# The high part of the first network's weights: written by VectorE behind its bit operation instead of by ScalarE

## The chip, the cores and the metric

One core of a Trainium2 chip runs the whole program in one launch. The metric is the device time of that launch in microseconds (us); the time before is the median of three runs, 988.29 us (987.73 to 989.37). Engines are named as the profile names them: PE (TensorE matmul), PEld (TensorE weight load), DVE (VectorE), ACT (ScalarE), POOL (GpSimd) and SP (SyncE, which only issues DMAs here).

## The reference

Attention over 4 batches of 8 heads, 576 positions and 64 features, is computed in two parts and added: over a window of 3 neighbours on either side, and over the means of 4 positions. The result `x` (2304 tokens by 512) goes through two networks:

```python
def _moe_ref(x, w_in, w_out):
    h = x @ w_in                # 512 -> 2048
    g = h * np.cos(h)
    return (g @ w_out)          # 2048 -> 512

def _moe2_ref(x, w_a, w_b, w_out):
    a = x @ w_a                 # 512 -> 1536
    b = x @ w_b
    return (a * b @ w_out)
```

Inputs and outputs are float32, and the output has to be near that in accuracy.

## The kernel before

**Products of split numbers.** TensorE multiplies in a shorter format (`F32R`) here, so each operand is split into a high part (a copy rounded to `F32R`) and a low part (what is left). `mm3` (lines 430 to 432) issues three matmuls per product: high by high, high by low, low by high.

**The first network** runs over token blocks of 288 (two of 432 at the end) and sixteen slices `f` of 128 hidden features. One step `g` of the main loop is one slice of one block: `h_mm` multiplies a slice of `w_in` with the block (12 matmuls into one of two PSUM buffers with the tag `h`), `cos_a` (lines 469, 470) and `cos_b` (474, 477, 478) make h·cos(h) in `gs`, `split_hi` (482, ACT) and `split_lo` (486, POOL for the first steps, DVE later) split it, and three steps behind `back_mm` multiplies it with a slice of `w_out` (12 matmuls into the accumulators `acc`). The cosine is a chain of five instructions that changes engines: ACT 469, DVE 470, ACT 474 (a sine), ACT 477 (a square), DVE 478. Line 478 is the last reader of the PSUM buffer, so the `h` matmuls of two steps later wait for it.

**The first network's weights** arrive once, in 32 slices of 128 x 512 (16 of `w_in`, 16 of `w_out`), as 8-byte numbers, and are turned into float32 on the core. For each slice `to_f32` issues two ACT instructions (lines 113 and 116) and one DVE bit operation (118, a shift and an or, which writes the float32 bit pattern `lw`); then `wsplit` writes the high part into `t[:, 0]` (line 125) and POOL subtracts for the low part (126). `lw` is every other 4-byte word of the slice's buffer. The main loop asks for slices by `goal(g)`: four before the first step, then two in each of the first seven steps, then slower, until all are there after step 23. The load of a slice waits for line 118 of the slice eight places ahead of it.

**Beside it runs attention** for the next block: DVE makes sums of four (190) and masked scores (228, 232, 233, 246), ACT takes exponentials (247, 255, 257, 262), DVE and POOL normalise (285 to 303), PE transposes (310, 319) and multiplies (329, 336).

**The order of the work.** Each engine runs its instructions in one fixed order. The program is written step by step, but the Tile framework chooses that order when it builds the kernel, by its own schedule; another instruction on an engine moves its neighbours too. From the last block of the first network on, the program's own order is kept. The second network (a Strassen-like product of splits of `w_a`, `w_b`, `w_out2`) fills the time from about 575 us to the end; the 24 slices of its weights that are prepared earlier go through `to_f32` as well, but not through `wsplit`.

Of the kernel before, what the change touches and what calls it, by code (L numbers as in the profile page):

```python
# [9 lines left out]
F32 = mybir.dt.float32  # L10
# [5 lines left out]
AF = mybir.ActivationFunctionType  # L16
# [51 lines left out]
def kernel(ctx, tc, qT, kT, vw, vds, w_in, w_out, w_a, w_b, w_out2, out):  # L68
    nc = tc.nc
    pe, act, dve, pool, sp = nc.tensor, nc.scalar, nc.vector, nc.gpsimd, nc.sync  # L70
# [40 lines left out]
    def to_f32(raw, out=None, behind=None):  # L111
        lw, hh = raw[:, :, 0], raw[:, :, 1]
        ins = act.activation(out=hh.bitcast(F32), in_=hh.bitcast(F32), func=AF.Prelu, scale=2.0 ** -112, alpha=2.0 ** 32)
        after(ins, behind)
        top = raw.rearrange("p f e -> p (f e)").bitcast(mybir.dt.uint8).rearrange("p (f b) -> p f b", b=8)[:, :, 3]
        ins = act.activation(out=lw, in_=top, func=AF.Identity, scale=1.0 / 32.0, bias=down[:, :1])
        after(ins, behind)
        ins = dve.scalar_tensor_tensor(out=lw if out is None else out, in0=hh, scalar=3, in1=lw, op0=ALU.logical_shift_left, op1=ALU.bitwise_or)  # L118
        marks.append(ins.ins)
        return lw  # L120

    def wsplit(raw, lo_eng):
        t = wp.tile([128, 2, 512], F32R, tag="w", name="w", bufs=33)
        lw = to_f32(raw)
        act.activation(out=t[:, 0], in_=lw.bitcast(F32), func=AF.Copy)
        lo_eng.tensor_tensor(out=t[:, 1], in0=lw.bitcast(F32), in1=t[:, 0].bitcast(F32), op=ALU.subtract)  # L126
        return t[:, 0], t[:, 1]

# [289 lines left out]
    def split_to(nm, f):  # L418
        while (nm, f) not in wts:
            key = stream[pos[1]]  # L420
            while pos[0] < len(stream) and pos[0] < pos[1] + C["AHEAD"]:
                load_next()
            wts[key] = wsplit(raws.pop(key), pool)
            pos[1] += 1
# [89 lines left out]
    if True:  # L514
# [227 lines left out]
        for g in range(NG + LAG):  # L742
            if g < NG:
                i, u, f = seq[g]
                if g == NG - NF:
                    at_ctx.close()
                    p2 = ctx.enter_context(tc.tile_pool(name="p2", bufs=1))
                    act, dve, pool = InOrder(tc, act), InOrder(tc, dve), InOrder(tc, pool)
# [289 lines left out]
```

## Time and profile before

| what | value |
|---|---|
| median of three runs | 988.29 us |
| the profiled execution's own time | 987.76 us |
| its span (first to last instruction) | 985.6 us |
| PE busy | 942.4 us (96%) |
| PE weight load busy | 892.4 us (91%) |
| DVE busy | 708.1 us (72%) |
| ACT busy | 609.9 us (62%) |
| POOL busy | 477.5 us (48%) |
| mean granted clock of TensorE | 0.979 of full speed |

The shares are means over the whole span. The stages differ much: the lines that the change touches run only in the first 160 us. "Busy" of PE counts a matmul from its start to its modelled end, so that PE is not necessarily at its peak where it is busy. "Idle before" of an engine is put down to the instruction that released it.

### The profile page before, as it was taken

To read this page: it belongs to the slowest core of one execution; us is meant where nothing else is said; L and a number is where in the kernel's file an instruction comes from. 1 tells how busy PE (TensorE), PEld (TensorE's weight loads), DVE (VectorE), ACT (ScalarE), POOL (GpSimd) and SP (SyncE) were. 2 spreads that over 40 slices of the span, in tenths; PEclk is the share of its full clock that TensorE was granted. 3 is DMA by queue.
4 is the path that set the end of the run, shared out by engine and by line. 5 is a ranking of instruction groups with operands and counts; after the bars stand their busy time and mean duration, and the time that the engine had idled before them with its cause. 6 is when DMAs were issued, how large, how long until landed. Compare 5 with 4: busy or idle time off the path is not lost.

```text
span 985.6 us, 18933 instructions
## 1 busy us (share of the span) xinstructions
PE 942.4 (96%) x6828; PEld 892.4 (91%) x6828; DVE 708.1 (72%) x1378; ACT 609.9 (62%) x1399; POOL 477.5 (48%) x615
## 2 busy tenths in 40 slices
PE   4888899999999999999999999999999999999998
PEld 3767898989889989899999989998999998999998
DVE  7677777577767777656346878889856789667773
ACT  5689897476675858676468765555444455444452
POOL 3757642014221351112015347658777769566682
PEclk8779999999999999999999999999999999999999
DMA  9646511244546363432049855576554685753431
GB/s 287 244 132 209 189 43 39 69 126 138 157 125 184 116 185 113 123 105 60 1 138 280 253 181 193 188 288 238 222 173 154 205 340 214 256 176 141 160 134 49
DMA packets 98829, 163.30 MB, mean 166 GB/s; under 512 B 6960, under 2 KB 64816, under 8 KB 98736
## 3 DMA queue, kind: packets, MB, share of 16 engines
q1 hardware_dynamic: 98736, 162.10, 49.7%
q8 instruction: 54, 0.88, 0.4%
q14 instruction: 39, 0.32, 0.1%
HBM read 128.25 MB, written 33.82 MB: 164 GB/s over the span
## 4 chain that ended last, share of the span: by engine, by line
PE 73%; DVE 10%; ACT 6%; DMA 5%; POOL 4%; issue 2%; SPq 0%; POOLq 0%; DVEq 0%; ACTq 0%
PE z L431 12%; PE z L432 12%; PE z L430 12%; PE h L430 5%; PE acc L430 5%; PE h L431 5%; PE h L432 5%; PE acc L432 5%; PE acc L431 5%; DMA vs<-in_vds_dram 2%; PE att L336 2%; PE att L217 1%; PE att L244 1%; POOL vd L183 1%; PE att L329 1%
## 5 line engine op out<-in xcount | busy, mean ns | idle before, releaser
L64 POOL TENSOR_TENSOR sb<-w,sb 128x256 fp32r<-128x256 f32 x154 | 120.7, 796 | 90.7 <-ACT sb L64 87.0
L430 PE MATMUL h<-xh,w 128*128 128x288 f32 (+1 forms) x448 | 146.7, 327 | 7.9 <-DVE gs L478 7.0
L430 PE MATMUL acc<-gh,w 128*128 128x288 f32 (+1 forms) x448 | 145.0, 325 | 2.0 <-DVE ev L463 1.0
L431 PE MATMUL acc<-gl,w 128*128 128x288 f32 (+1 forms) x448 | 142.3, 318 | 1.9 <-POOL gl L486 1.7
L432 PE MATMUL h<-xh,w 128*128 128x288 f32 (+1 forms) x448 | 142.1, 317 | 1.2 <-POOL w L126 1.2
L431 PE MATMUL h<-xl,w 128*128 128x288 f32 (+1 forms) x448 | 142.9, 319 | 0.0
L432 PE MATMUL acc<-gh,w 128*128 128x288 f32 (+1 forms) x448 | 141.9, 317 | 0.0
L64 ACT ACTIVATE sb<-w 128x256 fp32r<-128x256 f32 x252 | 96.4, 415 | 66.1 <-PE z L432 54.2
L430 PEld LDWEIGHTS h<-xh,w 128*128 128x128 f32 x448 | 85.6, 191 | 15.5 <-DVE gs L478 9.9
L432 PE MATMUL z<-xh,sb 128*128 128x384 f32 x288 | 97.4, 338 | 0.2 <-POOL sb L64 0.2
L430 PE MATMUL z<-xh,sb 128*128 128x384 f32 x288 | 96.9, 336 | 0.4 <-issue 0.4
L431 PE MATMUL z<-xl,sb 128*128 128x384 f32 x288 | 97.2, 338 | 0.0
L430 PEld LDWEIGHTS acc<-gh,w 128*128 128x128 f32 x448 | 85.1, 190 | 7.7 <-issue 2.9
L618 POOL TENSOR_TENSOR praw<-praw 128x128 f32<-128x128 f32 x24 | 12.8, 531 | 162.3 <-DVE praw L118 128.5
L431 PE MATMUL z<-gl,w 128*128 128x384 f32 x252 | 85.7, 340 | 4.4 <-DVE gl L64 4.1
L431 PEld LDWEIGHTS acc<-gl,w 128*128 128x128 f32 x448 | 85.2, 190 | 4.0 <-POOL gl L486 2.1
L432 PEld LDWEIGHTS h<-xh,w 128*128 128x128 f32 x448 | 86.0, 192 | 2.8 <-POOL w L126 1.5
L431 PEld LDWEIGHTS h<-xl,w 128*128 128x128 f32 x448 | 85.8, 192 | 1.9 <-issue 0.9
L432 PEld LDWEIGHTS acc<-gh,w 128*128 128x128 f32 x448 | 85.0, 190 | 2.4 <-issue 1.1
L430 PE MATMUL z<-gh,w 128*128 128x384 f32 x252 | 85.1, 338 | 0.1
L432 PE MATMUL z<-gh,w 128*128 128x384 f32 x252 | 84.9, 337 | 0.0
L64 DVE TENSOR_TENSOR sb<-w,sb 128x256 fp32r<-128x256 f32 x98 | 62.2, 637 | 26.5 <-ACT sb L64 26.4
(141 smaller groups left out, 2503.6 us busy)
## 6 DMA issues: line engine op xcount, KB each, us to landing
w<-wd SPq DMA_DIRECT2D x63, 512.0 KB
w<-wd_a SPq DMA_DIRECT2D x18, 512.0 KB
w<-wd_b SPq DMA_DIRECT2D x18, 512.0 KB
raw<-in_w_in_dram SPq DMA_DIRECT2D x16, 512.0 KB
raw<-in_w_out_dram SPq DMA_DIRECT2D x16, 512.0 KB
w<-wd_a SPq DMA_DIRECT2D x18, 384.0 KB
w<-wd_b SPq DMA_DIRECT2D x18, 384.0 KB
praw<-in_w_a_dram SPq DMA_DIRECT2D x12, 512.0 KB
```

The source lines that it names most:

```text
L64: return lambda *a, **k: self.tc.keep_in_program_order(f(*a, **k))
L183: pool.tensor_tensor(out=o, in0=t[:, :, 0], in1=t[:, :, 1], op=ALU.add)
L217: pe.matmul(p[r, W * w:W * w + W], qt[u, hp][r, off:off + W], kt[b, hp][r, BASE[half] + off:BASE[half] + off + W], start=not pem, stop=True,)
L244: pe.matmul(p[a][:QD, :SD], qd[u, hp][r, :], kd[b, hp][r, :], start=True, stop=True)
L329: pe.matmul(p[64 * a:64 * a + 64, NB:NB + QD], vdt[b, hp][:, a, c], pd[u, hp][:, 2 * a + c], start=(c == 0), stop=(c == 1),)
L336: pe.matmul(p[64 * a:64 * a + 64, xo:xo + n], vt[u, hp // 2][r, w, a], pt[u, hp // 2][r, w, 64 * a + qo:64 * a + qo + n], start=True, stop ...
L430: i = pe.matmul(ps_out, lh, rh, start=start, stop=False, skip_group_check=more)
L431: pe.matmul(ps_out, lh, rl, start=False, stop=False, skip_group_check=more)
L432: pe.matmul(ps_out, ll, rh, start=False, stop=stop, skip_group_check=more)
L618: pool.tensor_tensor(out=s1, in0=a21, in1=a22, op=ALU.add)
```

## The change

One line of `wsplit`: the high part is written by a DVE copy and not by an ACT activation.

```diff
     def wsplit(raw, lo_eng):
         t = wp.tile([128, 2, 512], F32R, tag="w", name="w", bufs=33)
         lw = to_f32(raw)
-        act.activation(out=t[:, 0], in_=lw.bitcast(F32), func=AF.Copy)
+        dve.tensor_copy(out=t[:, 0], in_=lw.bitcast(F32))
         lo_eng.tensor_tensor(out=t[:, 1], in0=lw.bitcast(F32), in1=t[:, 0].bitcast(F32), op=ALU.subtract)
         return t[:, 0], t[:, 1]
```

The copy is called CAST in the lists of instructions. 32 instructions leave ACT, and 32 come to DVE. Since the framework chooses the order anew, instructions beside them move on all engines: the order differs from about 29 us to about 165 us of the profile before, and not behind that.

ACT, from the first step's line 469 to its line 477 (the first cosine chain; `raw` are weight slices, `smd` scores of the means). Before:

```order
L469 ACTIVATE gs<-h 128x288
L247 ACTIVATE smd<-att,mxd 72x144
L113 ACTIVATE raw<-raw 128x512
L125 ACTIVATE w<-raw 128x512
L247 ACTIVATE smd<-att,mxd 72x144
L474 ACT_TABLE_LOAD
L474 ACTIVATE gs<-gs 128x288
L125 ACTIVATE w<-raw 128x512
L477 ACTIVATE gs<-gs 128x288
```

Now:

```order
L469 ACTIVATE gs<-h 128x288
L247 ACTIVATE smd<-att,mxd 72x144
L474 ACT_TABLE_LOAD
L474 ACTIVATE gs<-gs 128x288
L247 ACTIVATE smd<-att,mxd 72x144
L477 ACTIVATE gs<-gs 128x288
```

Two instructions of line 125 and one of line 113 no longer stand inside the chain (113 has moved ahead of it).

DVE, from line 470 to line 478 of the same chain. Before:

```order
L470 SCALAR_TENSOR_TENSOR gs<-gs,h 128x288
L233 TENSOR_TENSOR smx<-smx,mx 128x5x64
L118 SCALAR_TENSOR_TENSOR raw<-raw 128x512
L228 TENSOR_TENSOR smx<-att,mask 128x5x64
L232 TENSOR_REDUCE mx<-smx 128x5
L228 TENSOR_TENSOR smx<-att,mask 128x5x64
L233 TENSOR_TENSOR smx<-smx,mx 128x5x64
L232 TENSOR_REDUCE mx<-smx 128x5
L246 TENSOR_REDUCE mxd<-att 72x1
L233 TENSOR_TENSOR smx<-smx,mx 128x5x64
L478 SCALAR_TENSOR_TENSOR gs<-gs,h 128x288
```

Now:

```order
L470 SCALAR_TENSOR_TENSOR gs<-gs,h 128x288
L233 TENSOR_TENSOR smx<-smx,mx 128x5x64
L246 TENSOR_REDUCE mxd<-att 72x1
L125 CAST w<-raw 128x512
L228 TENSOR_TENSOR smx<-att,mask 128x5x64
L118 SCALAR_TENSOR_TENSOR raw<-raw 128x512
L232 TENSOR_REDUCE mx<-smx 128x5
L228 TENSOR_TENSOR smx<-att,mask 128x5x64
L478 SCALAR_TENSOR_TENSOR gs<-gs,h 128x288
```

One copy has come between them; two of line 233 and one of line 232 have gone behind line 478.

DVE, the normalising of the second block's scores, which lies between lines 470 and 478 of the third step. Its beginning, before:

```order
L470 SCALAR_TENSOR_TENSOR gs<-gs,h 128x288
L118 SCALAR_TENSOR_TENSOR raw<-raw 128x512 x2
L190 TENSOR_REDUCE kd<-k 128x144 x2
L285 TENSOR_REDUCE sl<-smx 128x10 x2
L286 TENSOR_SCALAR sl<-sl 128x10
```

Now:

```order
L470 SCALAR_TENSOR_TENSOR gs<-gs,h 128x288
L125 CAST w<-raw 128x512
L118 SCALAR_TENSOR_TENSOR raw<-raw 128x512
L125 CAST w<-raw 128x512
L118 SCALAR_TENSOR_TENSOR raw<-raw 128x512 x2
L285 TENSOR_REDUCE sl<-smx 128x10 x2
```

Two copies and one more bit operation stand ahead of line 285; two sums of line 190 have gone behind it. Its end, before:

```order
L303 TENSOR_TENSOR smd<-smd,sd 72x288
L190 TENSOR_REDUCE kd<-k 128x144
L297 TENSOR_SCALAR sd<-sd 72x2
L298 RECIPROCAL sd<-sd 72x2
L303 TENSOR_TENSOR smd<-smd,sd 72x288
L297 TENSOR_SCALAR sd<-sd 72x2
L298 RECIPROCAL sd<-sd 72x2
L303 TENSOR_TENSOR smd<-smd,sd 72x288
L478 SCALAR_TENSOR_TENSOR gs<-gs,h 128x288
```

Now:

```order
L125 CAST w<-raw 128x512
L298 RECIPROCAL sd<-sd 72x2
L190 TENSOR_REDUCE kd<-k 128x144
L303 TENSOR_TENSOR smd<-smd,sd 72x288
L297 TENSOR_SCALAR sd<-sd 72x2
L125 CAST w<-raw 128x512
L298 RECIPROCAL sd<-sd 72x2
L190 TENSOR_REDUCE kd<-k 128x144
L303 TENSOR_TENSOR smd<-smd,sd 72x288
L125 CAST w<-raw 128x512
L190 TENSOR_REDUCE kd<-k 128x144
L478 SCALAR_TENSOR_TENSOR gs<-gs,h 128x288
```

Four copies (three of them here, one two rows ahead) have come between the norms, and the next step's line 470 as well, four rows ahead of the piece; one sum of line 190 has gone behind line 478. Up to that line 478 the program now has written twelve high parts.

## Rows read from the trace of the kernel before

**Rows 1.** Busy time by stretch: from:to, length, then PE, PEld, DVE, ACT, POOL, PEclk, DMA.

```profile
0.00:30.00 30.00, 16.48 (x175) 12.71 (x176) 20.56 (x57) 16.59 (x46) 14.72 (x30) 0.76 0.94 306
30.00:68.00 38.00, 32.55 (x281) 25.62 (x279) 26.77 (x59) 29.16 (x72) 23.59 (x31) 0.74 0.48 166
68.00:98.00 30.00, 26.02 (x287) 23.73 (x286) 20.13 (x38) 28.39 (x64) 22.04 (x21) 1.00 0.62 200
98.00:165.00 67.00, 61.26 (x486) 57.24 (x486) 50.48 (x103) 58.34 (x134) 36.06 (x42) 0.97 0.29 91
165.00:985.60 820.60, 806.13 (x5610) 773.13 (x5608) 590.16 (x1122) 477.40 (x1088) 381.05 (x494) 1.00 0.50 165
...
50.00:59.50 9.50, 9.50 (x34) 7.55 (x34) 5.87 (x13) 6.40 (x14) 1.81 (x3) 0.50 0.73 245
```

**Rows 2.** What PE waited for from 68 to 98 us: total us, times, longest.

```profile
PE h L430 <- DVE gs L478: 3.2, 2, 2.1
PE h L432 <- POOL w L126: 0.6, 1, 0.6
```

**Rows 3.** Groups by form of ACT, 30 to 165 us: count, busy us, mean ns, idle before.

```profile
L116 ACT ACTIVATE raw<-raw,down 128x512 uint32<-128x512 uint8 x28 | 21.4, 766 | 0.1
L125 ACT ACTIVATE w<-raw 128x512 fp32r<-128x512 f32 x32 | 21.4, 672 | 3.2 <-DVE raw L118 2.3 <-POOL w L126 0.7
L113 ACT ACTIVATE raw<-raw 128x512 f32<-128x512 f32 x27 | 18.3, 679 | 0.0
```

**Rows 4.** Line 118 on DVE, 30 to 165 us: ns min/median/max.

```profile
L118 DVE SCALAR_TENSOR_TENSOR raw<-raw x28: 673/694/2165, 32.6 to 157.2; 128x512 uint32<-128x512 uint32 x28
```

**Rows 5.** Groups by form of DVE, 30 to 165 us.

```profile
L190 DVE TENSOR_REDUCE kd<-k 128x144 f32<-128x576 f32 x4 | 2.9, 737 | 0.0
L190 DVE TENSOR_REDUCE qd<-q 128x72 f32<-128x288 f32 x4 | 1.7, 442 | 0.0
L286 DVE TENSOR_SCALAR sl<-sl 128x10 f32<-128x10 f32 x4 | 0.6, 160 | 0.0
```

**Rows 6.** ACT in order of time, first cosine chain: start us, us, [idle before].

```profile
41.31 0.67 ACT L113 ACTIVATE raw<-raw 128x512 f32<-128x512 f32 x1
41.87 0.66 ACT L125 ACTIVATE w<-raw 128x512 fp32r<-128x512 f32 x1
...
44.46 0.66 ACT L125 ACTIVATE w<-raw 128x512 fp32r<-128x512 f32 x1
45.03 0.43 ACT L477 ACTIVATE gs<-gs 128x288 f32<-128x288 f32 x1
```

**Rows 7.** DVE in order of time, the same chain and the third step's.

```profile
41.35 0.44 DVE L470 SCALAR_TENSOR_TENSOR gs<-gs,h 128x288 f32<-128x288 int32 x1
41.71 1.39 DVE L233 TENSOR_TENSOR smx<-smx,mx 128x320 f32<-128x320 f32 x1
...
47.16 0.44 DVE L478 SCALAR_TENSOR_TENSOR gs<-gs,h 128x288 f32<-128x288 f32 x1
...
55.92 0.44 DVE L470 SCALAR_TENSOR_TENSOR gs<-gs,h 128x288 f32<-128x288 int32 x1
...
67.48 0.44 DVE L478 SCALAR_TENSOR_TENSOR gs<-gs,h 128x288 f32<-128x288 f32 x1
```

**Rows 8.** PE in order of time, what follows the two lines 478.

```profile
47.65 0.40 PE L430 MATMUL h<-xh,w 128*128 128x288 f32 x1 [1.53 <-DVE gs L478]
...
67.99 0.80 PE L336 MATMUL att<-smx,v 64*64 64x57 f32 x20
68.72 0.40 PE L430 MATMUL h<-xh,w 128*128 128x288 f32 x1
```

**Rows 9.** What PE waited for from 98 to 165 us.

```profile
PE h L430 <- DVE gs L478: 1.7, 2, 1.1
PE acc L431 <- POOL gl L486: 1.6, 1, 1.6
PE att L244 <- DVE smx L228: 1.0, 1, 1.0
```

**Rows 10.** POOL's line 126 over the span: duration ns min/median/max, and what POOL waited for.

```profile
L126 POOL TENSOR_TENSOR w<-raw,w x32: 1287/1318/1772, 33.5 to 158.7; 128x512 fp32r<-128x512 f32 x32
...
  ACT w L125: 20.5, 14
```

**Rows 11.** DVE and POOL in order of time around 117 us.

```profile
116.57 2.17 DVE L118 SCALAR_TENSOR_TENSOR raw<-raw 128x512 uint32<-128x512 uint32 x1 [0.21 <-DMA raw<-in_w_in_dram]
...
116.88 1.31 POOL L126 TENSOR_TENSOR w<-raw,w 128x512 fp32r<-128x512 f32 x1
```

## The prediction

> **What bounds the kernel now.** I read the busy time by stretch first, because the changed line runs only between 31 and 158 us. Behind 165 us PE is busy 806.1 of 820.6 us [rows 1]: that part is PE's own, the order there is unchanged, and it can only start sooner or later. So the question is how much sooner or later the stretch from 30 to 165 us ends. I cut it in three: I from 30 to 68 us, II from 68 to 98, III from 98 to 165. PE stands idle 5.5 us in I, 4.0 in II and 5.7 in III (length less busy, [rows 1]), 15.2 us together; no gain there can be larger, but for the clock, below. In II the engine that is busiest is not PE but ACT, 28.4 of 30 us, and next comes what PE waits for in that stretch: 3.2 us for line 478, the end of the cosine chain, and 0.6 us for a low part of the weights [rows 2]. Three of the chain's five instructions run on ACT and stand there in line behind weight conversion. In III ACT is 87% busy and DVE 75%; in I neither leads all the time.
>
> **What leaves ACT.** 32 instructions of 672 ns, 21.4 us [rows 3]: nine each in I and II, fourteen in III. ACT's waits in front of them (2.3 us for line 118) go with them. POOL, which waited 20.5 us for them [rows 10], now waits for DVE's copy instead; it has time.
>
> **What comes to DVE.** 32 copies of 128x512 float32 words. No row of before shows such a copy between two places of SBUF. The nearest is line 118, DVE's own pass over the same 512 words, 694 ns at the median [rows 4]; I take 0.69 us. A second row agrees: the reductions of line 190 take 442 ns for 288 words and 737 ns for 576 [rows 5], 1.02 ns a word, so 512 would take 0.67 us. The lower end is what an instruction costs that does nearly nothing, 0.16 us for ten words (line 286, [rows 5]). The upper end is 0.69 us plus a whole instruction of POOL, 1.32 us [rows 10], 2.0 us, which is near the longest line 118, 2165 ns [rows 4]. At 0.69 us DVE gets 22.1 us. The Trainium skill ("VectorE: DVE Perf Modes", the perf-mode tier table) says that a float32 copy within SBUF may run two words a cycle, and its cost table gives about 0.33 us for 512 words, an estimate; by it DVE would get 10.5 us and the sum below would be 5.3 us of gain and not 3.2. No row here shows that rate.
>
> **Stretch I.** The first cosine chain loses two of line 125 and one of line 113 on ACT. From start to start these take 1.1 us ahead of the table load and 0.57 us ahead of line 477 (41.31 to 42.4, 44.46 to 45.03, [rows 6]). So ACT's part ends 1.7 us sooner, at 43.8. DVE's part now holds line 233 (1.39 us, [rows 7]), one of 246, one copy, two of 228, one of 118 and one of 232 between lines 470 and 478: with 0.69 each for the copy and 118, 0.3 to 0.5 for the rest and some 0.08 of overlap, 4.2 us from 41.7, so line 478 starts at 45.9 and not at 47.16 [rows 7]. PE waited 1.53 us for it [rows 8] and starts 1.3 us sooner: **-1.3 us**.
>
> Then comes a part in which DVE alone sets the pace: from line 470 at 55.92 to line 478 at 67.48 [rows 7] it normalises scores. Into it come six copies (4.1 us), one more line 118 (0.7) and one line 470 (0.4), and one line 190 (0.7) leaves: 4.5 us more. It starts 1.3 us sooner, so this line 478 moves from 67.48 to 70.7. PE did not wait for it before: it was at line 336 until 68.7, and the next `h` matmul began at 68.72 [rows 8], 0.8 us behind the end of line 478. Now that matmul is late: 70.7 and 0.4 for the instruction make 71.1, **+2.4 us**. The cover (attention's matmuls on PE) is gone there. Stretch I together: +1.1 us.
>
> **Stretch II.** Nine copies' worth of work leaves ACT, 6.0 us. By the new order twelve high parts, not nine, are written by line 478 of the third step, so three slices less are converted here: 3 x (0.68 + 0.77) us less on ACT [rows 3], three of line 118 less on DVE, and six copies instead of nine. ACT: 28.4 - 6.0 - 4.3 = 18.0 us. DVE: 20.1 + 6 x 0.69 - 3 x 0.69 = 22.2 us. PE, 26.0 us [rows 1], becomes the busiest, and its waits (3.8 us, [rows 2]) have little left to wait for. I take 3.3 of its 4.0 idle us, since five steps in this stretch still hand over from engine to engine: **-3.3 us**; ends 0 and -4.0.
>
> **Stretch III.** ACT falls by 9.4 to 48.9 us, DVE rises by 9.7 to 60.1 of 67 us: DVE now has the share (90%) that ACT had. PE waits 1.7 us for line 478, 1.6 for a low part on POOL and 1.0 for scores on DVE [rows 9]. The last two gain nothing from a lighter ACT. I take **-1.0 us** of the first; ends +2 and -2.7.
>
> **Loads** cost nothing: their issue waits on line 118 of an earlier slice, and that line's own wait for data in the whole stretch is 0.2 us [rows 11].
>
> Sum: +1.1 - 3.3 - 1.0 = -3.2 us. The profiled execution took 987.76 us, 0.53 below the median of 988.29; taken from the median, **985.1 us**.
>
> **The rivals.** *A, the sum above, likeliest.* Its own range is 981 to 987.5.
>
> *B, a cheap copy and a full PE.* If the copy costs near its lower end of 0.16 us, the normalising part grows by 1.4 us and starts 1.3 sooner, so stretch I keeps its -1.3; II gives all of its 4.0 and III 2.3: -7.6 us, 980.7. Beyond it lies the clock: from 50 to 59.5 us it was granted at 0.50, the lower of its two levels (1.2 of 2.4 GHz), against 1.00 in II [rows 1]; a PE with shorter waits ahead of that might keep the upper one for longer. For it: PE's longest waits hang on ACT's queue. Against: no copy so cheap is in the trace.
>
> *C, the load only changes engines.* DVE takes 22 us where ACT loses 21, the chain of five waits in one line instead of the other, and nothing moves: 988.3. For it: in III DVE ends at ACT's old share. Against: in II the two do not balance, 22.2 against 28.4 us.
>
> *D, slower: the copy and POOL's subtraction lock each other out.* Line 118 at 116.57 took 2.17 us instead of 0.69, and POOL's line 126 ran inside it, 1.31 us [rows 11]: DVE instructions with such operands wait for POOL's to end. The copy's consumer is just this line 126, started when the copy ends, with the next line 118 or copy right behind on DVE. DVE's 97.4 us of 30 to 165 (26.8 + 20.1 + 50.5, [rows 1]) and 22.1 for copies make 119.5 of 135; at a packing of 95% (ACT's in II) DVE binds from 128 on, so from a mean wait of 0.27 us per copy. If every second copy waits a whole 1.32 us, that is 21 us: 140.6, 5.6 more than the stretch has: 993.9. The Trainium skill ("SBUF — State Buffer", Who interferes with whom) states this as a rule: a copy in a two-port mode and a GpSimd instruction exclude each other for an instruction's whole length. By that rule a cheap copy is just the one that gets locked out; the trace agrees as to line 118, and for a copy no run shows it yet. Against D: the median of line 118 is 694 ns, so most pass freely, and POOL is busy only 60% of the time.
>
> That the change does not do what it says is excluded by the order: 32 copies stand on DVE, none of line 125 on ACT.
>
> **How the numbers follow.** Chances: A 0.45, B 0.17, C 0.16, D 0.22. A measurement of this kernel can tell about 0.2%, 2.0 us, from no change: faster is below 986.3, slower above 990.3. A lies in the faster part with 0.36 and within 0.2% with 0.09; B is faster; C is within; D is slower. So 0.53 faster, 0.25 the same, 0.22 slower. The range takes half of B and half of D: 979 to 993; A's own stands above.
>
> **What would show it.** Right: ACT near 18 us and PE over 28 us in the 27 us or so that follow the third step's line 478, which itself ends near 71 us with PE waiting for it; the end of line 126's run near 155 us and not 160; copies at 0.3 to 0.8 us. Wrong: copies of over 1 us in the mean, with POOL's line 126 beside them (D); a third step's line 478 no later than 68 us (B); or PE's idle time of 30 to 165 us still near 15 us, with other names in front (C).

## The result and the profile after

The changed kernel takes 995.08 us (median of five runs, 993.32 to 997.57); the kernel before, run beside it, 987.73 us. The ratio is 1.0061, with a 95% interval of 1.0031 to 1.0090: **slower, by 6.0 us** (3.1 to 8.9); the medians alone differ by 7.4 us. Differences in microseconds below are worked out from the ratios in the same way. The forecast was 985.1 us with a range of 979 to 993; the result lies outside it, on the side of rival D. The profiled execution took 995.08 us, its span 993.3 us.

The busy time by stretch of the changed kernel, columns as in [rows 1]; the last line is the 27 us behind the third step's line 478:

```profile
0.00:30.00 30.00, 17.53 (x176) 13.51 (x177) 21.08 (x58) 16.75 (x46) 14.75 (x30) 1.00 0.93 314
30.00:68.00 38.00, 31.00 (x232) 24.55 (x231) 29.34 (x64) 26.33 (x64) 25.87 (x30) 0.87 0.55 201
68.00:98.00 30.00, 28.30 (x255) 26.26 (x255) 27.36 (x41) 23.67 (x55) 25.79 (x22) 0.82 0.52 185
98.00:165.00 67.00, 55.08 (x450) 50.45 (x449) 55.21 (x116) 45.42 (x100) 34.41 (x40) 1.00 0.23 69
165.00:993.30 828.30, 814.46 (x5724) 781.22 (x5722) 594.20 (x1134) 484.43 (x1104) 383.63 (x496) 1.00 0.49 164
...
72.30:99.30 27.00, 25.30 (x222) 23.81 (x221) 24.36 (x36) 21.77 (x51) 22.43 (x20) 0.88 0.58 206
```

ACT is lighter, as meant: 45.4 us in stretch III, not 58.3. But PE is busy 55.1 of those 67 us, not 61.3 [rows 1]; from 30 to 165 us its idle time grew from 15.2 to 20.6 us. TensorE's lower clock, 0.50, came at other times, but that does not explain the loss: over the whole of 30 to 165 us the granted clock is 0.92 in both profiles (last column but two), first before, then changed:

```profile
30.00:165.00 135.00, 119.82 (x1048) 106.59 (x1047) 97.38 (x199) 115.90 (x267) 81.69 (x92) 0.92 0.42 136
...
30.00:165.00 135.00, 114.38 (x933) 101.26 (x932) 111.92 (x219) 95.43 (x217) 86.06 (x90) 0.92 0.38 132
```

In stretch III, where the loss will turn out to lie, the changed kernel even has the higher one, 1.00 against 0.97.

When does the loss come? The start of line 469 (ScalarE's timeline) marks each step. The tenth and the twenty-sixth step, first of the kernel before, then of the changed one:

```profile
98.34 0.41 ACT L469 ACTIVATE gs<-h 128x288 int32<-128x288 f32 x1
...
163.78 0.41 ACT L469 ACTIVATE gs<-h 128x288 int32<-128x288 f32 x1 [0.45 <-PE h L432]
...
99.60 0.38 ACT L469 ACTIVATE gs<-h 128x288 int32<-128x288 f32 x1
...
173.54 0.41 ACT L469 ACTIVATE gs<-h 128x288 int32<-128x288 f32 x1 [0.58 <-PE h L432]
```

So the changed kernel is 1.3 us late at the tenth (it was 1.4 us late at the very first) and 9.8 us late at the twenty-sixth. Some 2 us of that come back behind 165 us: the span is longer by 7.7. The loss arises in stretch III.

What PE waits for from 98 to 165 us (total, times, longest):

```profile
PE h L430 <- DVE gs L478: 5.4, 5, 1.8
PE acc L430 <- DVE ev L463: 3.5, 3, 2.1
PE att L217 <- DVE smx L228: 2.0, 1, 2.0
PE att L244 <- ACT smd L247: 0.6, 1, 0.6
PE att L319 <- DVE sl L286: 0.4, 1, 0.4
```

Four of five names are DVE's, 11.3 us together; before, line 478 had 1.7 us [rows 9]. Now the instructions of the conversion, from 25 to 175 us: ns min/median/max, then first and last start:

```profile
L118 DVE SCALAR_TENSOR_TENSOR raw<-raw x28: 678/1314/1930, 31.8 to 142.2; 128x512 uint32<-128x512 uint32 x28
...
L125 DVE CAST w<-raw x32: 408/426/1526, 29.4 to 144.8; 128x512 fp32r<-128x512 f32 x32
...
  POOL w L126: 6.2, 3
...
L126 POOL TENSOR_TENSOR w<-raw,w x32: 1289/1314/1840, 33.4 to 145.3; 128x512 fp32r<-128x512 f32 x32
```

The copy itself is cheap, 0.43 us at the median and 0.64 us in the mean (20.4 us together). Line 118, which the change doesn't touch, went from a median of 0.69 us [rows 4] to 1.31: from 23.7 us (28 times 850 ns) to 34.3 us (28 times 1226). That is 10.5 us of DVE's time that the forecast has not. The line under the copy is a third thing: three times, 6.2 us in all, DVE stood idle in front of a copy until line 126 of an earlier slice freed one of the 33 buffers that `raw` and `w` share.

The timelines show why line 118 is slow (start, duration, engine). First DVE, then POOL:

```profile
87.69 0.41 DVE L125 CAST w<-raw 128x512 fp32r<-128x512 f32 x1
88.02 0.44 DVE L470 SCALAR_TENSOR_TENSOR gs<-gs,h 128x288 f32<-128x288 int32 x1
88.39 1.72 DVE L118 SCALAR_TENSOR_TENSOR raw<-raw 128x512 uint32<-128x512 uint32 x1
90.14 0.92 DVE L125 CAST w<-raw 128x512 fp32r<-128x512 f32 x1
90.99 0.44 DVE L478 SCALAR_TENSOR_TENSOR gs<-gs,h 128x288 f32<-128x288 f32 x1
91.35 1.65 DVE L118 SCALAR_TENSOR_TENSOR raw<-raw 128x512 uint32<-128x512 uint32 x1
...
88.23 1.32 POOL L126 TENSOR_TENSOR w<-raw,w 128x512 fp32r<-128x512 f32 x1 [1.38 <-ACT gh L482]
...
91.14 1.31 POOL L126 TENSOR_TENSOR w<-raw,w 128x512 fp32r<-128x512 f32 x1 [0.36 <-PE acc L431]
```

The copy ends, POOL's line 126 starts on what it wrote, and DVE's next line 118, an instruction with two operands in SBUF, falls into it and ends 0.55 or 0.56 us after it: 1.72 and 1.65 us in place of 0.68. Of the 28 line 118s, 15 take over 1.1 us here. Each of the 15 ends 0.54 to 0.56 us behind a two-operand GpSimd instruction, 14 times line 126 and once line 370. Before it was 5 of 28; two of these had a line 126 beside them (one is in [rows 11]) and the other three a line 370 or 486, two-operand instructions of GpSimd as well. There ACT wrote the high part, with a queue of its own in between, and a line 126 overlapped 9 of the 28 line 118s, not 22 as here. The long copies have the same mark: all 13 that take over 0.6 us end 0.28 or 0.29 us behind a two-operand GpSimd instruction.

### The profile page after: what moved, and what is told of

Same layout as the page of the kernel before. It is cut to its first block, busy times and chain, and to the rows that moved or that the text cites. A ratio compares the mean times of both kernels' runs of the same rounds, so it can differ in the third digit from the quotient of the medians.

```text
span 993.3 us, 18940 instructions
## 1 busy us (share of the span) xinstructions
PE 946.4 (95%) x6828; PEld 896.0 (90%) x6828; DVE 727.2 (73%) x1410; ACT 596.6 (60%) x1367; POOL 484.4 (49%) x615
## 4 chain that ended last, share of the span: by engine, by line
PE 70%; DVE 8%; ACT 4%; DMA 3%; POOL 2%; issue 1%; SPq 0%; DVEq 0%; POOLq 0%; ACTq 0%
PE z L431 12%; PE z L432 12%; PE z L430 12%; PE h L430 5%; PE acc L430 5%; PE h L431 5%; PE h L432 5%; PE acc L432 4%; PE acc L431 4%; PE att L336 1%; DMA vs<-in_vds_dram 1%; PE att L217 1%; DMA y_dram<-ev 1%; PE att L244 1%; DVE gl L64 1%
## 5 line engine op out<-in xcount | busy, mean ns | idle before, releaser
L430 PEld LDWEIGHTS acc<-gh,w 128*128 128x128 f32 x448 | 84.4, 189 | 11.8 <-DVE ev L463 4.5
```

The source lines that it names most:

```text
L430: i = pe.matmul(ps_out, lh, rh, start=start, stop=False, skip_group_check=more)
```

## The experiments

Theories. **P**: VectorE's two-operand line 118 and its copy and GpSimd's two-operand line 126 exclude each other. **R**: the copy's wait for a free buffer, in VectorE's own queue. **L**: the mere load on VectorE. **O**: the order that the framework chose anew. All ratios are to the kernel before.

| run | edit | ratio (95%) |
|---|---|---|
| e1_first18 | copies on DVE for slices 1 to 18 only | 1.0018 (0.9991 to 1.0045) |
| e2_last14 | copies on DVE for slices 19 to 32 only | 1.0076 (1.0048 to 1.0103) |
| e3_first24 | copies on DVE for slices 1 to 24 only | 1.0075 (1.0050 to 1.0099) |
| e6_memset | changed kernel, line 126 a fill | 0.9884 (0.9841 to 0.9928) |
| e7_before_memset | kernel before, line 126 a fill | 0.9909 (0.9873 to 0.9945) |
| e12_memset3 | changed kernel, line 126 three fills | 0.9963 (0.9943 to 0.9983) |
| e11_pool1in | changed kernel, line 126 reads `lw` alone | 0.9942 (0.9920 to 0.9964) |
| e14_pooldep | changed kernel, line 126 reads the high part alone | 0.9942 (0.9923 to 0.9961) |
| e20_before_pooldep | kernel before, the same | 0.9936 (0.9911 to 0.9960) |
| e8_reduce | the copy as a one-input reduction | 1.0015 (0.9993 to 1.0038) |
| e16_red18 | that for slices 1 to 18, ACT for the rest | 0.9994 (0.9972 to 1.0016) |
| e17_dve_odd | kernel before, every second line 126 on DVE | 1.0032 (1.0007 to 1.0058) |
| e18_dve_lo | kernel before, all of line 126 on DVE | 0.9882 (0.9860 to 0.9904) |
| e19_dve_both | changed kernel, all of line 126 on DVE | 0.9951 (0.9928 to 0.9973) |

### Where the loss lies: some copies on each engine

```diff
-        dve.tensor_copy(out=t[:, 0], in_=lw.bitcast(F32))
+        if pos[1] < 18:
+            dve.tensor_copy(out=t[:, 0], in_=lw.bitcast(F32))
+        else:
+            act.activation(out=t[:, 0], in_=lw.bitcast(F32), func=AF.Copy)
```

The other two have `pos[1] >= 18` and `pos[1] < 24`.

> The first 18 of the 32 high parts are written by VectorE, the last 14 by ScalarE as before. The changed kernel started its step 9 only about 1 us later than the kernel before and its step 18 about 11 us later, so the loss lies where the last 14 slices are converted. Theory P (VectorE's copy and its line 118 and GpSimd's line 126 exclude each other, and this costs where VectorE is full): most of the loss goes, -2 to +2 us against the kernel before; line 118's mean falls from 1.23 us toward the 0.85 us of before for the late slices. Theory R (the copy waits in VectorE's queue for a free weight buffer, 6.2 us in three places, all after the 24th slice): these three waits go, -1 to +3 us. Theory L (the mere busy time of 32 copies at 0.43 us): 14 of 32 parts of the loss of 6 us go, so +3.4 us stay. Theory O (the order that the framework chose anew costs it, wherever the copies are): +5 us or more may stay.

> The converse: the first 18 high parts on ScalarE as before, the last 14 on VectorE. P and R: the loss is here, +4 to +10 us against the kernel before, with VectorE's line 118 over 1.2 us in the mean for the late slices (P) or with VectorE idle for over 4 us in front of line 125, waiting for GpSimd's line 126 (R). L: +2.6 us. O: cannot say; where the sum of this run's and the other's difference is far from the whole change's +6 us, the two parts act on each other.

> The first 24 of the 32 high parts on VectorE, the last 8 on ScalarE. The copy waited for a free weight buffer only behind the 24th slice (6.2 us in three places), so here VectorE has none of these waits, but 24 of the 32 meetings of copies and line 118 with GpSimd's line 126. Theory R (those waits are the loss): -1 to +2 us against the kernel before, with no idle VectorE in front of the copies. Theory P (mutual exclusion with line 126): +3 to +6 us, with line 118 over 1.1 us in the mean while VectorE makes copies. The run with the first 18 gave +1.8 us (-0.9 to +4.5) and the one with the last 14 gave +7.6 us (+4.8 to +10.3), so here both would say +2 to +5 where they mix.

The first 18 slices cost 1.8 us (-0.9 to 4.5), the last 14 alone 7.5 (4.8 to 10.2): the loss is with the late ones, as the step times say. L's share of 3.4 us would fit the first, its 2.6 us doesn't fit the second. P's own sign was missed in both: the late line 118s (from 98 us on) take 1.08 us in the mean in the first run and 1.01 in the second, where 0.85 and over 1.2 had been expected, and the second has R's sign, 4.3 us of idle DVE in front of the copies. So these two do not choose between P and R. The third run tests R. Its copies, and under them the empty list of what DVE waited for in front of one:

```profile
L126 DVE CAST w<-raw x24: 410/608/1526, 29.5 to 112.7; 128x512 fp32r<-128x512 f32 x24
...
its engine sat idle before it (us, times) until:
who waited for it (us, times):
```

No copy waits for a buffer, and the loss is there whole, 7.4 us (P had said 3 to 6): **R falls** as the main cause (ACT's late copies wait 3.8 us for line 126 instead, but not in DVE's queue). Its line 118 takes 1.13 us in the mean, hardly more than the 1.12 of the first run with its 1.8 us, so the summed length of line 118 does not by itself give the loss. These kernels have an order of their own; they give the place and not the size.

### Is it the subtraction? Fills in its place

```diff
-        lo_eng.tensor_tensor(out=t[:, 1], in0=lw.bitcast(F32), in1=t[:, 0].bitcast(F32), op=ALU.subtract)
+        lo_eng.memset(t[:, 1].bitcast(F32), 0.0)
```

In the changed kernel this leaves the order of DVE, ACT and SP as it is, row by row. The third of these kernels issues the fill three times.

> The changed kernel, with GpSimd's subtraction (line 126) replaced by a fill with zeros of the same tile, so the low part of the first network's weights is left out. A fill reads nothing and should be much shorter than 1.3 us and should keep VectorE out for less. P: the copies fall to about 0.43 us in the mean, line 118 to about 0.7 to 0.85 us, and the loss goes: within 2 us of the same edit made in the kernel before. R: the wait for a free buffer shrinks too, but line 118 keeps its 1.2 us. L and O: the kernel stays 5 to 7 us above the same edit made in the kernel before, with copies of 0.64 us.

> The control: the same fill with zeros in the kernel before (low part of the first network's weights left out). P: line 118 falls from 0.85 us in the mean to about 0.7 us, the time by 0 to 3 us against the kernel before. All theories: it tells what the subtraction itself costs when ScalarE writes the high part; 985 to 988 us.

> The changed kernel with line 126 replaced by three fills with zeros, 0.52 us each, so GpSimd is busy 1.57 us per slice, more than with the subtraction (1.31 us), without reading what VectorE wrote; the low part of the first network's weights is left out. The order is near that of the changed kernel, not the same. P: the loss does not come back, 978 to 984 us, with line 118 at 0.7 to 0.85 us in the mean. The rival to P is that GpSimd's time itself delays buffers and hand-overs: then the time returns to 988 to 996 us.

With the fill the loss is gone: 11.5 us faster than the kernel before, and, against the same edit there, 0.9975 (the errors of the two ratios added in squares: 0.992 to 1.003). Line 118 in the changed kernel with the fill:

```profile
L118 DVE SCALAR_TENSOR_TENSOR raw<-raw x29: 673/693/957, 24.4 to 125.1; 128x512 uint32<-128x512 uint32 x29
```

So **O falls**: the changed order, without the subtraction, is no slower than the old one. One expectation was missed: the copies did not fall to 0.43 us in the mean but stayed at 0.61 (19.6 us together, not 20.4), some as long as in the changed kernel:

```profile
L125 DVE CAST w<-raw x32: 409/418/1748, 29.7 to 126.8; 128x512 fp32r<-128x512 f32 x32
```

The loss is gone all the same, so the long copies alone are not what costs it. Unexpected was how much the subtraction costs in the kernel before: 9.0 us. Three fills keep POOL busier than the subtraction (52.7 us against 45.4, as the groups by line have it) and still give 0.9963, with line 118 at 0.74 us in the mean: POOL's time is not the cause. That is 7.8 us more than one fill (3.1 to 12.5), so POOL's length, or the slightly other order on PE and POOL, has some price too.

### Only the number of operands

```diff
-        lo_eng.tensor_tensor(out=t[:, 1], in0=lw.bitcast(F32), in1=t[:, 0].bitcast(F32), op=ALU.subtract)
+        lo_eng.tensor_scalar(out=t[:, 1], in0=t[:, 0].bitcast(F32), scalar1=0.0, scalar2=None, op0=ALU.mult)
```

The first run of this kind reads `lw` (`in0=lw.bitcast(F32)`), so that it doesn't wait for the copy; the others read the high part.

> The changed kernel with line 126 replaced by a GpSimd multiplication of one input (lw) by zero, so the low part of the first network's weights is left out. VectorE's, ScalarE's and the loads' order is that of the changed kernel but for a few loads. It reads the same words as the subtraction, but one operand, and does not wait for the copy. P: whether line 118 and the copies are kept out as with the subtraction tells whether one input is enough; if so, line 118's mean is 1.0 us or more and the loss stays in part (+0 to +6 us against the kernel before, and clearly above the run with the fill, 979.7 us). If line 118 falls to 0.7 to 0.75 us and the copies to 0.42 us, the time is near that run, 978 to 982 us. O (the new order costs it): excluded by the fill with zeros already, which ran in the changed kernel's VectorE and ScalarE order without the loss.

> The changed kernel with line 126 replaced by a GpSimd multiplication by zero of one input, the high part that the copy has just written; the low part of the first network's weights is left out. Every engine has the order of the changed kernel, row by row; GpSimd still waits for the copy, and its instruction should take 1.5 us or more (the one that read lw took 1.51 at the least, 1.73 in the mean). Only the number of operands read differs. P (two instructions with two operands each exclude each other): line 118's mean is 0.7 to 0.85 us and the time 978 to 985 us, as with the multiplication that did not wait for the copy (-5.8 us against the kernel before). The rival Q (what the earlier runs without the loss had in common is that the low part no longer hung on the copy, so that the row of bit operation, copy and subtraction was cut): the time stays 990 us or more although line 118 is short.

> The kernel before with line 126 as a GpSimd multiplication by zero of one input, the high part that ScalarE has just written; the low part of the first network's weights is left out. Every engine keeps the order of the kernel before. The same edit made the changed kernel 5.7 us faster than the kernel before. If the change itself is worth what was forecast once the exclusion is away (3.2 us): -1 to -4 us here, with line 118 at 0.72 to 0.75 us. If the change is worth nothing even then: -5 to -7 us. If it costs something apart from the exclusion: -8 us or more.

In the first run the loss is gone already (0.9942), with line 118 at 0.84 us in the mean and copies at 0.55, but there POOL no longer waits for the copy. It also answers R once more, for DVE still stands idle in front of copies until line 126 frees a buffer:

```profile
L125 DVE CAST w<-raw x32: 408/478/1040, 29.1 to 130.2; 128x512 fp32r<-128x512 f32 x32
...
  POOL w L126: 3.8, 3
```

The second is the clean test of the number of operands: every engine has the changed kernel's order, POOL waits for the copy as before, its instruction is longer, and one operand less is read. From 25 to 175 us:

```profile
L118 DVE SCALAR_TENSOR_TENSOR raw<-raw x29: 673/693/1476, 24.7 to 130.0; 128x512 uint32<-128x512 uint32 x29
...
L125 DVE CAST w<-raw x32: 409/417/998, 29.3 to 131.8; 128x512 fp32r<-128x512 f32 x32
...
L126 POOL TENSOR_SCALAR w<-w x32: 1480/1499/3057, 32.1 to 136.7; 128x512 fp32r<-128x512 f32 x32
```

Line 118's median is back at 0.69 us, its mean at 0.81, and the ratio is 0.9942, 11.8 us below the changed kernel (1.0061). **P is shown**, and the rival Q (the row of bit operation, copy and subtraction) falls. No copy waits for a buffer here, since line 126 no longer reads `raw`; that this is not what brings the time back is said by the first run, where 3.8 of the 6.2 us of such waits were left. DVE and POOL of this run, some 5 us ahead of the rows of the changed kernel above:

```profile
82.25 0.68 DVE L118 SCALAR_TENSOR_TENSOR raw<-raw 128x512 uint32<-128x512 uint32 x1
82.85 0.44 DVE L478 SCALAR_TENSOR_TENSOR gs<-gs,h 128x288 f32<-128x288 f32 x1
83.21 0.47 DVE L125 CAST w<-raw 128x512 fp32r<-128x512 f32 x1
83.59 0.45 DVE L470 SCALAR_TENSOR_TENSOR gs<-gs,h 128x288 f32<-128x288 int32 x1
84.15 0.69 DVE L118 SCALAR_TENSOR_TENSOR raw<-raw 128x512 uint32<-128x512 uint32 x1
...
82.25 3.95 POOL L126 TENSOR_SCALAR w<-w 128x512 fp32r<-128x512 f32 x2
```

Two line 118s run at full speed inside two POOL instructions, and it is these that become longer (1.98 us each, not 1.50). Not always: of the 13 line 118s that began inside a line 126, ten took 0.68 to 0.73 us and three 0.84 to 1.08, such as

```profile
112.91 1.07 DVE L118 SCALAR_TENSOR_TENSOR raw<-raw 128x512 uint32<-128x512 uint32 x1
...
111.06 3.26 POOL L126 TENSOR_SCALAR w<-w 128x512 fp32r<-128x512 f32 x2 [0.43 <-ACT raw L113]
```

In the changed kernel 11 began inside a line 126, and all 11 took over 1 us.

The third run gives the price of the exclusion in the kernel before: 0.9936, 6.3 us. So the exclusion costs 6.3 us (2.4 either way) before and 11.8 us (3.5 either way) after; the difference, 5.5 us, is nearly the whole of the change's 6.0, though with an error of some 4 us. And without it the change is worth nothing: 0.9942 over 0.9936 is 1.0006, +0.6 us, 3.1 either way. The forecast of 3.2 us of gain was answered by "worth nothing even then".

### The copy as a one-input reduction

```diff
-        dve.tensor_copy(out=t[:, 0], in_=lw.bitcast(F32))
+        dve.tensor_reduce(out=t[:, 0], in_=lw.bitcast(F32).unsqueeze(2), axis=AX.X, op=ALU.max)
```

> The changed kernel with the copy written as a maximum over an axis of length one (a VectorE reduction with one input), which by the rows of line 190 costs about 0.67 us for 512 words. P, if only the fast form of the copy is kept out by line 126: these instructions take 0.6 to 0.75 us each and never 1.4 us, though VectorE's time for them, 21 us, is as much as the copies took with their waits (20.4 us); line 118 keeps its 1.2 us; the time stays +3 to +8 us. L (mere load): it grows by 32 x 0.25 = 8 us more, +10 to +14 us. If reductions of 1.4 us or more appear beside line 126, any VectorE instruction of this length is kept out, whatever its form.

> A version that may beat both: the first 18 high parts by the one-input reduction on VectorE (never longer than 0.69 us in the run with all 32), the last 14 by ScalarE as before. In the run with all 32 reductions the steps up to the eleventh started up to 6 us sooner than before and lost it again behind that. P: -5 to 0 us against the kernel before, with line 118 at 0.9 to 1.05 us in the mean. If what is gained in the early steps is owed back by attention, which then comes later: -1 to +2 us.

The reductions in the first of them:

```profile
L125 DVE TENSOR_REDUCE w<-raw x32: 657/674/689, 29.2 to 139.0; 128x512 fp32r<-128x512 f32 x32
```

None is kept out, while the copies ran from 0.41 to 1.53 us. They take 21.5 us of DVE against 20.4, and line 118 falls only to 1.03 us in the mean; yet the time is 1.5 us above before (-0.7 to 3.8), not the 3 to 8 that P had named, and far from L's 10 to 14. A copy that is never slow, though never fast, is no worse. How much of this is the other order that the framework made of it stays open. The Trainium skill ("SBUF — State Buffer", Who interferes with whom) says that a reduction never contends with GpSimd on this chip, a copy can, and a two-input instruction does with one that reads; with line 126 reading two operands, as here, the rows agree in all three. The mixed version (0.9994) beats nothing.

### The subtraction on VectorE

```diff
-        lo_eng.tensor_tensor(out=t[:, 1], in0=lw.bitcast(F32), in1=t[:, 0].bitcast(F32), op=ALU.subtract)
+        dve.tensor_tensor(out=t[:, 1], in0=lw.bitcast(F32), in1=t[:, 0].bitcast(F32), op=ALU.subtract)
```

In the first run for every second slice only (`dve if pos[1] % 2 else lo_eng`).

> The kernel before (ScalarE writes the high part) with every second low part subtracted on VectorE and not on GpSimd. The fill with zeros in place of the subtraction made the kernel before 9 us faster, so GpSimd's subtraction costs even there. P: line 118 falls from 0.85 us in the mean to about 0.77, VectorE gets 16 x 0.7 us = 11 us more; -4 to +2 us against the kernel before. If VectorE's load is what counts and not the exclusion: +1 to +5 us.

> The same with all 32 low parts on VectorE: line 126 leaves GpSimd altogether. P: line 118 near 0.72 us in the mean; VectorE gets 22 us of subtractions (0.7 us each) and loses 4 us of line 118, as much new load as the copies and their waits brought in the changed kernel, but nothing to be kept out by: -5 to +3 us. L (load on VectorE is what costs): +5 to +9 us, as the changed kernel or more.

> The changed kernel with the subtraction on VectorE too: bit operation, copy and subtraction stand on one engine, GpSimd has no part of it. VectorE gets 0.42 us (copy) and 0.72 us (subtraction) per slice, 36 us in all. The kernel before with the subtraction on VectorE ran at 0.9882, 979.9 us. If taking the copy from ScalarE is worth something without the exclusion: 973 to 979 us. If VectorE's load now binds (97 + 36 us of 135 us between 30 and 165 us, less 10 us that line 118 loses): 981 to 988 us.

With all 32 on DVE the kernel before gains 11.7 us: 0.9882, **979.88 us, the version that beats both kernels**, with nothing left out. Its lines 118 and 126:

```profile
L118 DVE SCALAR_TENSOR_TENSOR raw<-raw x28: 670/693/1195, 32.3 to 147.1; 128x512 uint32<-128x512 uint32 x28
...
L126 DVE TENSOR_TENSOR w<-raw,w x32: 672/684/944, 31.6 to 148.8; 128x512 fp32r<-128x512 f32 x32
```

DVE takes on 23.0 us of subtraction (32 times 720 ns), more than the copies' 20.4, and the kernel is faster. So it was not load as such. The gain is more than the 6.3 us that the exclusion costs this kernel; GpSimd is also relieved here, and what that is worth no run shows alone. With half of them on DVE it is 3.2 us slower: POOL's half still meets DVE, which now has more two-operand instructions (its own subtractions reach 1.72 us, line 118 0.92 in the mean); this I had not expected. And with the copy on DVE as well the gain shrinks to 4.8 us:

```profile
68.00:98.00 30.00, 27.56 (x257) 25.52 (x256) 27.77 (x53) 24.67 (x58) 13.16 (x13) 0.84 0.48 169
98.00:165.00 67.00, 64.94 (x578) 61.25 (x577) 61.77 (x148) 49.64 (x115) 17.50 (x25) 1.00 0.29 90
```

DVE is busy 27.8 of 30 and 61.8 of 67 us there (third number). Against the same kernel with the copy on ACT the change costs 0.9951 over 0.9882, 0.7%, 6.9 us (3.1 either way), without any exclusion by line 126. That is what L says, and it may hold once DVE is this full; no run isolates it.

## Why the prediction was wrong

**The sum itself** counts 1.3 us twice. The 70.7 us of the third step's line 478 already holds the earlier start, so the +2.4 behind it is all of stretch I, and taking 1.3 off again to get +1.1 is an error. By its own terms the sum is -1.9 and the forecast 986.4 us. That would still be a gain.

**Stretch I, +1.1 forecast.** The first chain failed: line 478 began at 48.70 us, not 45.9. The step that put line 118 at 0.69 us there failed; in the changed kernel's timeline it took 1.73 us, and shortly ahead of it DVE stood idle 1.61 us for PE's scores of line 217. The third step's line 478 began at 72.31, forecast "near 71".

**Stretch II, -3.3.** PE was busy 28.3 of 30 us and not 26.0, less than the 29.3 of the sum; ACT 21.8 of the 27 us behind that line, not 18. ("PE over 28 us in the 27 us or so" cannot be; it measures 25.3 there.) By the step times stretches I and II together came out at +1.3 us, the tenth step's delay, where -2.2 was forecast. If attention's work moved behind the tenth step, a part of that was owed; the step times alone can't tell.

**Stretch III, -1.0, ends +2 and -2.7.** Here the forecast broke: it lost some 8.5 us from the tenth to the twenty-sixth step. The working added 9.7 us of copies to DVE, saw 90% and took PE's waits for line 478 as shrinking; they grew from 1.7 to 5.4 us, and line 463 came to them with 3.5.

**The failed step** is that the sum put the exclusion by GpSimd's line 126 at nothing: it kept line 118 at its price of before, although the change puts line 126's start right in front of it, and so took PE's waits on DVE in stretch III as shrinking. What the runs show in its place is an exclusion of 11.8 us in the changed kernel and 6.3 in the kernel before. The copy itself was priced well, 0.69 us against a measured 0.64; the 0.33 us that the prediction gave by the Trainium skill's cost table ("VectorE: DVE Perf Modes") lies below even the shortest copy, 0.41. Line 118 was not: the sum has it at 0.69 us, and its mean was 0.85 before and is 1.226 now. A second step failed with it. Even without the exclusion the change gains nothing (+0.6 us, 3.1 either way), so the gain of 3.2 us from a lighter ACT was not there; why, stays open.

**Rival D** named the mechanism, and its reason against itself (the median of line 118 before) was a median under ACT's spacing, which the change removes. That its 993.9 us lies so near the result is partly luck. D had every second copy wait 1.32 us, 21 us in all, and DVE binding from 128 us of the 135 on; the copies took 0.64 us in the mean, far from the "over 1 us" that was to show D, and DVE was busy only 111.9 us, less than the 119.5 of the sum without any waits. Line 118 took the larger part, and other two-operand instructions of DVE got shorter, lines 233 above all, before and after, from 25 to 175 us:

```profile
L233 DVE TENSOR_TENSOR smx<-smx,mx 128x320 f32<-128x320 f32 x8 | 7.9, 990 | 0.0
...
L233 DVE TENSOR_TENSOR smx<-smx,mx 128x320 f32<-128x320 f32 x8 | 4.2, 533 | 0.0
```

Over the whole span DVE's busy time rose by 19.1 us (708.1 to 727.2), less than the 22.1 forecast. And the version with the subtraction on VectorE keeps DVE busy 110.3 us from 30 to 165 us, nearly as long as here, and is 11.7 us faster than the kernel before. So DVE's total did not make the loss. That it depends on where the exclusion strikes, ahead of the chain's lines 470 and 478 as in the rows around 90 us, is argued from those rows and not shown by a run.

**The other rivals.** B fails: most copies are cheaper than the sum's 0.69 us (0.43 at the median), though not as cheap as B's 0.16, and PE still waits. C (the load only changes engines) describes the kernel without the exclusion, +0.6 us with 3.1 either way. The loss through free buffers (6.2 us of DVE's idle time) was not foreseen; the run with 24 copies shows that the loss stands without it, not that it is free.

**Still open**: how the 5.5 us come about between line 118 and PE's waits, since line 118's summed length does not give them; what the 14 late slices have that the first 18 lack; and where the 2 us regained behind 165 us come from.

## What to carry to other kernels

An instruction moved to an engine brings its consumer's start with it: look at which instruction stands right behind it, and whether that one and the consumer can run side by side. Here the busy times said that VectorE had room, and it had; the loss came from an instruction that the change did not touch, held back by the moved one's consumer. Where GpSimd and VectorE each run instructions with two operands, price the pair by the trace's overlapping rows, and try the work on one engine: 23 us more on VectorE made the kernel before 11.7 us faster.

## What the runs showed of the hardware

A GpSimd instruction with two operands held back VectorE's two-operand instruction until it ended (1.72 us instead of 0.68, ending 0.56 us behind line 126); in the changed kernel all 11 line 118s that began inside a line 126 took over 1 us. One with a single operand mostly did not, though it is longer (1.50 us): ten of 13 ran in 0.68 to 0.73 us, and the GpSimd instruction grew, to 1.98 us where two were met. The Trainium skill ("SBUF — State Buffer", Who interferes with whom) has a two-input VectorE instruction contend with any GpSimd instruction that reads. The rows agree that the two contend, but with one operand it was mostly the GpSimd instruction that paid: line 118 took 0.81 us in the mean against 1.23. In the changed kernel with a fill, which reads nothing, line 118 took 0.96 us at the most. Copies between two places of SBUF, 512 float32 words of 8-byte stride, took 0.41 us when nothing kept them out, and up to 1.75 beside fills and two-operand instructions.
